# Softcap attention and a gated feed-forward layer: the gate as a tanh straight out of PSUM, gate and value units in turn, and outputs by chunks

## The chip, the cores and the metric

The kernel runs on one core of a Trainium2 chip. The core has engines that each work through a queue of their own in order: TensorE (PE; its weight loads are PEld in the profile), VectorE (DVE), ScalarE (ACT), GpSimd (POOL) and SyncE (SP), which here only issues DMAs. PE accumulates into banks of PSUM; ACT and DVE read these; everything else lives in SBUF. The metric is device time in microseconds.

## The reference

All arrays are float32, and the layer follows the attention directly:

```python
# q, k, v: (4, 12, 448, 64); w_gate, w_val: (768, 1536); w_out: (1536, 768)
scores = matmul(q, k.T) / sqrt(64)
scores = cap * tanh(scores / cap)               # cap = 30
attn = softmax(scores)
x = matmul(attn, v) -> (4*448, 12*64)           # tokens x model
gate = 1 / (1 + exp(-(x @ w_gate)))
val = x @ w_val
out = (gate * val) @ w_out                      # (1792, 768)
```

## The kernel before

Every float32 matrix is split into a high and a low half, and a product is three matmuls: high by low, high by high, low by high. A value that is made on the chip therefore passes two more engines before PE can use it: the high half is made by POOL or ACT (L174, L176), the low half, which subtracts it, by DVE (L182).

The attention takes a pair of heads at a time. PE transposes q and k (`tp`, L209 and L295), ACT copies them (`T`), PE makes the scores (`sc`, L325), ACT applies tanh to them (`t`, L328) and then exp (L336), ACT and DVE split the result (`ph`, `pl`), PE multiplies by v (`pv`, L366, L375 to L377). ACT copies parts of the product (`tmp`, L398), DVE adds (`xraw`, L400), POOL and DVE make the row sums (`a`, `as`), and DVE divides (`rd`). Six pairs make one batch of 448 tokens; DVE's `xspl` then holds its split x.

The feed-forward part of one batch, `moe(b)`, has 24 units h of 18 matmuls: 12 blocks of 128 columns of the gate and 12 of the values. Each unit ends in one of three PSUM banks. Then come two halves of the output, each of six units of w_out, with three chunks of 128 tokens that use the same three banks. The last 64 tokens of every batch are put off and done with the last batch (`rest`, `osr`).

The order of PE and ACT is the order of the program: the main loop takes turns between `moe(b)` and the attention of batch b+1, whichever is behind by its count of matmuls, so that a stretch of the profile holds both. A scheduler orders DVE, POOL and SP by dependences and by priorities (`tc.high_priority`). In the first such stretch the weights are also converted from 64-bit input by ACT and DVE (`pair`, L622 to L625) and written to DRAM; later batches load them back.

Around the change: the units are taken in three groups of four gate units and four value units. For a gate unit ACT copies the PSUM bank into a tile `gate` of four units (L749); after the fourth, one sigmoid goes over the whole tile (L755). For a value unit DVE multiplies the bank by the gate (L751), in the tile, and POOL and DVE split the product into `gspl` (L174, L182). The tile has one buffer, so the next group's first copy waits until the last low half of the old group is made. Tile `osb` of the output, three chunks wide, takes the same buffer. A sigmoid isn't in the table of functions that ACT holds for tanh and exp, so an `ACT_TABLE_LOAD` stands ahead of it, and another ahead of the next exp or tanh.

Of the kernel before, what the change touches and what calls it, by code (L numbers as in the profile page):

```python
# [9 lines left out]
F32 = mybir.dt.float32  # L10
# [5 lines left out]
AF = mybir.ActivationFunctionType  # L16
ALU = mybir.AluOpType
AX = mybir.AxisListType

P = 128  # L20
# [3 lines left out]
AHEAD_OF = 400  # L24
# [534 lines left out]
def _emit(tc, ctx, c, attention_of, q, k, v, w_gate, w_val, w_out, out):  # L559
# [3 lines left out]
    DFF = w_gate.shape[1]  # L563
    KD = DM // P
    KF = DFF // P
    NG = 3
    HM = DM // 2
    KU = 2
    W64 = 3
# [1 line left out]
    KEEP = 3  # L571
    AHEAD = 3
    WB = 4
    GF = KF // NG

    big = ctx.enter_context(tc.tile_pool(name="big", bufs=1))
    wp = ctx.enter_context(tc.tile_pool(name="wp", bufs=2))
# [5 lines left out]
    ap = o.ap  # L583
# [4 lines left out]
    UN = KD * P  # L588
    NU = 3 * KF
    src = []  # L590
    for g in range(NG):
        for w in (w_gate, w_val):
            for f in range(g * GF, (g + 1) * GF):
                src.append(w[:, f * P:(f + 1) * P].rearrange("(k p) f -> p k f", p=P))
    for t in range(2):
        wt = w_out[:, t * HM:(t + 1) * HM].rearrange("(k p) f -> p k f", p=P)
        for x in range(0, KF, KU):
# [103 lines left out]
    def next_w(u):  # L701
        if u < NU:
            convert_to(u + LEAD)
        split_w(u + AHEAD)
        load_to(u + WB)
        return w_spl.pop(u)

    def moe(b):
# [3 lines left out]
        def passes(ps, s):  # L712
            for kk in range(KD):
                rh, rl = xs[:, 0, kk, :], xs[:, 1, kk, :]
                wh, wl = (s[:, i, kk * P:(kk + 1) * P] for i in range(2))
                for i, (a, r) in enumerate(((wh, rl), (wh, rh), (wl, rh))):
                    nc.tensor.matmul(  # L717
                        ps, a, r, start=(kk == 0 and i == 0), stop=(kk == KD - 1 and i == 2)
                    )
                if kk % 2 == 1:  # L720
                    yield 6
# [13 lines left out]
                    )  # L735
                rest.append(r)
        u = u0
        for g in range(NG):
            gate = big.tile([P, GF, S], F32, tag="gate", name=f"gate{b}_{g}")
            for which in range(2):  # L740
                for j in range(GF):
                    f = g * GF + j
                    w = next_w(u)
                    u += 1
                    ps = ps_m.tile([P, S], F32, tag="m", name=f"h{b}_{which}_{f}")
                    yield from passes(ps, w)
                    gt = gate[:, j, :]
                    if which == 0:
                        nc.scalar.activation(gt, ps, AF.Copy)  # L749
                    else:  # L750
                        nc.vector.tensor_mul(gt, ps, gt)  # L751
                        o.hi("p", g_spl[:, 0, f, :], gt)
                        o.lo("v", g_spl[:, 1, f, :], gt, g_spl[:, 0, f, :])
                if which == 0:
                    nc.scalar.activation(gate, gate, AF.Sigmoid)  # L755
        moe1_done[b] = True
        flush_x()

# [19 lines left out]
        for t in range(2):  # L778
            acc = []
            for m in range(len(chunks)):  # L780
                if m < o.NF:
                    acc.append(ps_m.tile([P, HM], F32, tag="m", name=f"o{b}_{t}_{m}"))
                else:
                    acc.append(o.two_banks(f"o{b}_{t}_{m}")[:, 0, 0:HM])
            for x in range(0, KF, KU):
                w = next_w(u)
                u += 1
                for ps, g_of in zip(acc, chunks):
                    for kk in range(KU):
                        wh, wl = (w[:, i, kk * HM:(kk + 1) * HM] for i in range(2))  # L790
                        gh, gl = (g_of(i, x + kk) for i in range(2))
                        for i, (a, r) in enumerate(((gh, wl), (gh, wh), (gl, wh))):
                            nc.tensor.matmul(  # L793
                                ps, a, r, start=(x + kk == 0 and i == 0),
                                stop=(x + kk == KF - 1 and i == 2),
                            )
                    yield 3 * KU * HM / S
            to = out[:, t * HM:(t + 1) * HM]
            osb = big.tile([P, o.NF, HM], F32, tag="gate", name=f"osb{b}_{t}")
            for m, ps in enumerate(acc):  # L800
                if m == o.NF:
                    tag, bufs = o.out_tag
                    osb = ap.tile([P, NR // P, HM], F32, tag=tag, bufs=bufs, name=f"osr{b}_{t}")
                dst = osb[:, m % o.NF, :]
                if m % 2 == 0 or b < B - 1:

                    with tc.high_priority(offset=2 * AHEAD_OF):
                        nc.vector.tensor_copy(dst, ps)  # L808
                else:
                    nc.scalar.activation(dst, ps, AF.Copy)  # L810
                if m == o.NF - 1:
                    nc.sync.dma_start(
                        out=to[b * S:b * S + o.FULL].rearrange("(m p) e -> p m e", p=P), in_=osb
                    )
            if b == B - 1:
                ends = to.rearrange("(b s) e -> b s e", s=S)[:, o.FULL:]
                for m in range(NR // P):
                    nb = P // R
                    nc.sync.dma_start(out=ends[m * nb:(m + 1) * nb], in_=osb[:, m, :])


    MS = {mybir.EngineType.PE, mybir.EngineType.Activation}
# [59 lines left out]
```

## Time and profile before

| | |
|---|---|
| timed runs | 791.04, 793.67, 794.62 us; median 793.67 |
| the profiled execution | 791.81 us, of it a span of 789.5 us |
| busy in the span | PE 750.8 us (95%), DVE 472.6 (60%), ACT 398.6 (50%), POOL 198.0 (25%) |
| granted clock of PE | 0.983 of full speed on average |

The span has these stretches: to 85 us attention of batch 0 alone; then attention of batch b+1 beside the feed-forward part of batch b, from 85 to 278.7, to 451.1 and to 624.9 us; then the feed-forward part of the last batch, to PE's last matmul at 776.6; then the last outputs. In a row, an idle time in brackets is that of the row's engine just before it, with what ended it. A name such as `gate<-h` gives the tile written and the tile read, and x12 says that twelve instructions in succession are put together.

### The profile page before, as it was taken

What the parts mean: (1) busy time and instruction counts of PE and PEld (TensorE: products, weight loads), DVE (VectorE), ACT (ScalarE), POOL (GpSimd) and SP (SyncE); (2) the same over time, 40 slices, a digit from 0 to 9 for tenths busy, and PEclk for the clock granted to TensorE, in tenths of its full rate; (3) what the DMA queues carried; (4) which work ended last, traced back from release to release, by engine and by line L of the source; (5) the groups of instructions that cost most, each with busy time, mean ns of one, the idle gap of its engine ahead of it and who ended that gap; (6) DMA issues with size and microseconds to landing.
All of it is one profiled execution on the core that took longest, in us unless ns stands there. A gap on an engine that the chain in (4) does not pass through costs nothing.

```text
span 789.5 us, 10148 instructions
## 1 busy us (share of the span) xinstructions
PE 750.8 (95%) x3908; PEld 643.4 (81%) x3908; DVE 472.6 (60%) x525; ACT 398.6 (50%) x415; POOL 198.0 (25%) x211
## 2 busy tenths in 40 slices
PE   7999799999999999999999999999979999999993
PEld 4555587788777988887899988887879999999993
DVE  1689359888799948758798629667896011211000
ACT  6998377887756547674854256583830021010000
POOL 1133101020131325344465314434571000100000
PEclk9999799999999999999999999999999999999997
DMA  8777567999989876555577965543469866665521
GB/s 222 190 215 222 183 209 250 358 296 333 293 254 363 304 253 172 193 182 174 164 220 226 296 198 158 193 158 124 157 199 291 302 224 220 226 225 172 191 100 54
DMA packets 133170, 173.00 MB, mean 219 GB/s; under 512 B 86136, under 2 KB 111224, under 8 KB 133112
## 3 DMA queue, kind: packets, MB, share of 16 engines
q1 hardware_dynamic: 132184, 172.02, 67.9%
q8 instruction: 33, 0.54, 0.3%
q10 hardware_dynamic: 928, 0.23, 0.1%
q14 instruction: 25, 0.20, 0.1%
HBM read 135.27 MB, written 36.18 MB: 217 GB/s over the span
## 4 chain that ended last, share of the span: by engine, by line
PE 68%; DVE 15%; ACT 8%; issue 4%; POOL 2%; DMA 1%; SPq 0%; DVEq 0%; POOLq 0%; ACTq 0%
PE h L717 32%; PE o L793 19%; PE pv L366 6%; PE sc L325 5%; DVE pair L625 2%; DVE rd L418 2%; PE tp L209 2%; ACT t L328 2%; DVE wspl L182 2%; PE pv L375 1%; PE pv L376 1%; ACT gate L755 1%; DVE gspl L182 1%; ACT ph L176 1%; DVE pair L624 1%
## 5 line engine op out<-in xcount | busy, mean ns | idle before, releaser
L717 PE MATMUL h<-xspl,wspl 128*128 128x448 f32 x1728 | 380.2, 374 | 0.0
L717 PEld LDWEIGHTS h<-xspl,wspl 128*128 128x128 f32 x1728 | 323.8, 189 | 42.7 <-issue 15.0
L793 PE MATMUL o<-wspl,gspl 128*128 128x384 f32 x864 | 160.5, 340 | 1.1 <-DVE gate L751 0.8
L793 PEld LDWEIGHTS o<-wspl,gspl 128*128 128x128 f32 x864 | 151.8, 189 | 5.8 <-issue 3.5
L328 ACT ACTIVATE t<-sc,scale 112x896 f32<-112x896 f32 (+1 forms) x96 | 91.4, 1002 | 37.2 <-PE sc L325 36.7
L749 ACT ACTIVATE gate<-h 128x448 f32<-128x448 f32 x48 | 25.9, 542 | 156.8 <-PE h L717 97.0
L174 POOL TENSOR_SCALAR gspl<-gate 128x448 fp32r<-128x448 f32 x48 | 34.8, 724 | 204.8 <-DVE gate L751 204.8
L336 ACT ACTIVATE t<-t,capv 112x1792 f32<-112x1792 f32 (+1 forms) x48 | 85.7, 1789 | 0.4
L325 PE MATMUL sc<-T 64*112 64x448 f32 (+1 forms) x576 | 74.7, 387 | 9.6 <-DVE T L182 5.4
L366 PE MATMUL pv<-t,vo 112*128 112x448 f32 x192 | 78.6, 542 | 0.0
L325 PEld LDWEIGHTS sc<-T 64*112 64x112 f32 (+1 forms) x576 | 48.8, 180 | 34.9 <-issue 9.2
L418 DVE RECIPROCAL rd<-rd 128x448 f32<-128x448 f32 x24 | 70.8, 2951 | 0.3
L751 DVE TENSOR_TENSOR gate<-h,gate 128x448 f32<-128x448 f32 x48 | 29.5, 614 | 67.7 <-PE h L717 67.4
L348 POOL TENSOR_TENSOR a<-t 128x448 f32<-128x448 f32 x24 | 31.2, 1298 | 117.9 <-ACT t L336 90.2
L366 PEld LDWEIGHTS pv<-t,vo 112*128 112x128 f32 x192 | 35.4, 189 | 25.2 <-issue 24.6
L808 DVE COPY osb<-o 128x384 f32<-128x384 f32 x22 | 11.8, 553 | 72.6 <-PE o L793 72.5
L182 DVE TENSOR_TENSOR gspl<-gate,gspl 128x448 fp32r<-128x448 f32 x48 | 37.8, 788 | 24.3 <-POOL gspl L174 24.0
L182 DVE TENSOR_TENSOR pl<-t,ph 128x1344 fp32r<-128x1344 f32 x24 | 48.1, 2004 | 5.4 <-ACT ph L176 5.0
L176 ACT ACTIVATE ph<-t 128x1792 fp32r<-128x1792 f32 x24 | 40.7, 1697 | 18.1 <-PE pv L377 15.7
L623 DVE TENSOR_SCALAR pair<-pair 128x768 int32<-128x768 int32 x36 | 20.6, 573 | 38.7 <-ACT pair L622 37.2
L182 DVE TENSOR_TENSOR T<-tp,T 128x896 fp32r<-128x896 f32 (+1 forms) x24 | 26.9, 1121 | 25.7 <-ACT T L176 25.6
L622 ACT ACTIVATE pair<-w 128x768 f32<-128x768 f32 x36 | 32.5, 902 | 18.0 <-DVE wspl L182 12.1
(68 smaller groups left out, 728.2 us busy)
## 6 DMA issues: line engine op xcount, KB each, us to landing
wspl<-wd SPq DMA_DIRECT2D x111, 768.0 KB, 4.5
wd<-wspl SPq DMA_DIRECT2D x36, 768.0 KB, 5.3
w<-in_moe_w_gate_dram SPq DMA_DIRECT2D x12, 768.0 KB, 5.0
w<-in_moe_w_val_dram SPq DMA_DIRECT2D x12, 768.0 KB, 5.2
w<-in_moe_w_out_dram SPq DMA_DIRECT2D x12, 768.0 KB, 7.3
qk<-in_q_dram SPq DMA_DIRECT2D x46, 112.0 KB, 4.6
out_dram<-osb SPq DMA_DIRECT2D x8, 576.0 KB, 6.4
qk<-in_k_dram SPq DMA_DIRECT2D x22, 112.0 KB, 3.3
```

The costliest lines, as they stand in the source:

```text
L174: self.nc.gpsimd.tensor_scalar(dst, src, 1.0, 1.0, ALU.mult, ALU.mult)
L176: self.nc.scalar.activation(dst, src, AF.Copy)
L182: e.tensor_sub(dst, src, hi.bitcast(F32))
L325: nc.tensor.matmul(ps[0:w, j, 0:S], a[rows], r[rows], start=(i == 0), stop=(i == len(ops) - 1))
L328: nc.scalar.activation(Pt[n][0:w, :, m, :], ps[0:w, :, 0:S], AF.Tanh, scale=c["scale"][0:w])
L336: nc.scalar.activation(t, t, AF.Exp, scale=c["cap"][rows])
L348: nc.gpsimd.tensor_add(a, t[:, 0, :], t[:, 1, :])
L366: nc.tensor.matmul(pv, vs[n][0:QC, j * NC + m, :], Pt[n][0:QC, j, m, :], start=(m == 0), stop=(m == NC - 1),)
L418: nc.vector.reciprocal(rd, rd)
L622: nc.scalar.activation(x, top.bitcast(F32), AF.Copy, scale=2.0 ** -112)
L717: nc.tensor.matmul(ps, a, r, start=(kk == 0 and i == 0), stop=(kk == KD - 1 and i == 2))
L793: nc.tensor.matmul(ps, a, r, start=(x + kk == 0 and i == 0), stop=(x + kk == KF - 1 and i == 2),)
```

## The change

The sigmoid is written as (1 + tanh(x/2))/2, and tanh is in the table that ACT holds already. ACT reads a gate unit's bank once, with tanh and a scale of 0.5, and its tile holds one unit, with three buffers. DVE adds 1 and multiplies by the value unit's bank in one instruction, with raised priority. The factor 1/2 is applied when the output is copied out of PSUM. Units take turns, gate and value of the same block, and the weights are loaded in that order. The output's three chunks each have a tile of the ring `gate` and a DMA of their own.

```diff
-    for g in range(NG):
+    for f in range(KF):
         for w in (w_gate, w_val):
-            for f in range(g * GF, (g + 1) * GF):
-                src.append(w[:, f * P:(f + 1) * P].rearrange("(k p) f -> p k f", p=P))
+            src.append(w[:, f * P:(f + 1) * P].rearrange("(k p) f -> p k f", p=P))
...
-        for g in range(NG):
-            gate = big.tile([P, GF, S], F32, tag="gate", name=f"gate{b}_{g}")
+
+        for f in range(KF):
+            gate = big.tile([P, S], F32, tag="gate", bufs=3, name=f"gate{b}_{f}")
             for which in range(2):
-                for j in range(GF):
-                    f = g * GF + j
-                    w = next_w(u)
-                    u += 1
-                    ps = ps_m.tile([P, S], F32, tag="m", name=f"h{b}_{which}_{f}")
-                    yield from passes(ps, w)
-                    gt = gate[:, j, :]
-                    if which == 0:
-                        nc.scalar.activation(gt, ps, AF.Copy)
-                    else:
-                        nc.vector.tensor_mul(gt, ps, gt)
-                        o.hi("p", g_spl[:, 0, f, :], gt)
-                        o.lo("v", g_spl[:, 1, f, :], gt, g_spl[:, 0, f, :])
+                w = next_w(u)
+                u += 1
+                ps = ps_m.tile([P, S], F32, tag="m", name=f"h{b}_{which}_{f}")
+                yield from passes(ps, w)
                 if which == 0:
-                    nc.scalar.activation(gate, gate, AF.Sigmoid)
+                    nc.scalar.activation(gate, ps, AF.Tanh, scale=0.5)
+                else:
+                    with tc.high_priority(offset=AHEAD_OF):
+                        nc.vector.scalar_tensor_tensor(gate, gate, 1.0, ps, ALU.add, ALU.mult)
+                    o.hi("p", g_spl[:, 0, f, :], gate)
+                    o.lo("v", g_spl[:, 1, f, :], gate, g_spl[:, 0, f, :])
...
-            osb = big.tile([P, o.NF, HM], F32, tag="gate", name=f"osb{b}_{t}")
...
+                if m < o.NF:
+                    dst = big.tile([P, HM], F32, tag="gate", bufs=3, name=f"osb{b}_{t}_{m}")
+                else:
+                    dst = osr[:, m - o.NF, :]
                 if m % 2 == 0 or b < B - 1:
 
                     with tc.high_priority(offset=2 * AHEAD_OF):
-                        nc.vector.tensor_copy(dst, ps)
+                        nc.vector.tensor_scalar(dst, ps, 0.5, None, ALU.mult)
                 else:
-                    nc.scalar.activation(dst, ps, AF.Copy)
-                if m == o.NF - 1:
-                    nc.sync.dma_start(
-                        out=to[b * S:b * S + o.FULL].rearrange("(m p) e -> p m e", p=P), in_=osb
-                    )
+                    nc.scalar.activation(dst, ps, AF.Copy, scale=0.5)
+                if m < o.NF:
+                    at = b * S + m * P
+                    nc.sync.dma_start(out=to[at:at + P], in_=dst)
```

ACT's order in the feed-forward part of batch 1, from the end of the second group of gate units on, before (`h_0_6` is the gate unit of block 6):

```order
L749 ACTIVATE gate_1_2655<-h_0_6_2754 128x448
L749 ACTIVATE gate_1_2655<-h_0_7_2801 128x448
L755 ACT_TABLE_LOAD
L755 ACTIVATE gate_1_2655<-gate_1_2655 128x1792
L398 ACTIVATE tmp_0_2839<-pv_0_2808 64x448
L176 ACTIVATE ph_1_2842<-t_2535 128x1792
L328 ACTIVATE t_2769<-sc_2_2855,scale 128x2x448
L328 ACTIVATE t_2769<-sc_3_2863,scale 128x2x448
L176 ACTIVATE T_2904<-tp_2895 128x960
L336 ACT_TABLE_LOAD
L336 ACTIVATE t_2769<-t_2769,capv 128x1792
```

The same pair of heads in ACT's order after the change:

```order
L744 ACTIVATE gate_5_2770<-h_0_5_2773 128x448
L398 ACTIVATE tmp_0_2860<-pv_0_2827 64x448
L176 ACTIVATE ph_1_2863<-t_2552 128x1792
L328 ACTIVATE t_2788<-sc_2_2876,scale 128x2x448
L328 ACTIVATE t_2788<-sc_3_2884,scale 128x2x448
L744 ACTIVATE gate_6_2850<-h_0_6_2853 128x448
L176 ACTIVATE T_2923<-tp_2914 128x960
L336 ACTIVATE t_2788<-t_2788,capv 128x1792
```

Ahead of `tmp_0` there is one tanh of one unit where two copies, a table load and the sigmoid stood; another stands ahead of `T`, and no load stands ahead of the exp.

ACT's order one pair of heads later, before, where the third group begins:

```order
L415 ACTIVATE rd_2978<-dn_2975 128x448
L336 ACTIVATE t_2769<-t_2769,capv 128x1792
L328 ACTIVATE t_3003<-sc_0_3004,scale 128x2x448
L328 ACTIVATE t_3003<-sc_1_3012,scale 128x2x448
L749 ACTIVATE gate_2_3035<-h_0_8_3038 128x448
L398 ACTIVATE tmp_0_3075<-pv_0_3045 64x448
L176 ACTIVATE ph_1_3078<-t_2769 128x1792
L328 ACTIVATE t_3003<-sc_2_3091,scale 128x2x448
```

The same place after the change:

```order
L415 ACTIVATE rd_2998<-dn_2995 128x448
L744 ACTIVATE gate_7_2970<-h_0_7_2973 128x448
L336 ACTIVATE t_2788<-t_2788,capv 128x1792
L328 ACTIVATE t_3021<-sc_0_3022,scale 128x2x448
L328 ACTIVATE t_3021<-sc_1_3030,scale 128x2x448
L744 ACTIVATE gate_8_3053<-h_0_8_3056 128x448
L398 ACTIVATE tmp_0_3093<-pv_0_3063 64x448
L176 ACTIVATE ph_1_3096<-t_2788 128x1792
L328 ACTIVATE t_3021<-sc_2_3109,scale 128x2x448
```

The instruction of block 8 has kept its slot; it writes a tile of its own ring now, not the group's only one.

DVE's order before, in the feed-forward part of batch 2, where the last value units end and w_out begins (`gate_2` is the last group's tile, `h_1_9` the value unit of block 9):

```order
L751 TENSOR_TENSOR gate_2_4568<-h_1_9_4794,gate_2_4568 128x448
L182 TENSOR_TENSOR as_1_4846<-a_1_4841,as_1_4846 64x448
L182 TENSOR_TENSOR gspl_3843<-gate_2_4568,gspl_3843 128x448
L751 TENSOR_TENSOR gate_2_4568<-h_1_10_4826,gate_2_4568 128x448
L182 TENSOR_TENSOR gspl_3843<-gate_2_4568,gspl_3843 128x448
L751 TENSOR_TENSOR gate_2_4568<-h_1_11_4882,gate_2_4568 128x448
L182 TENSOR_TENSOR xspl_4904<-xraw_3908,xspl_4904 128x448 x4
L352 TENSOR_TENSOR a_0_4932<-a_0_4932 64x448
L182 TENSOR_TENSOR gspl_3843<-gate_2_4568,gspl_3843 128x448
L182 TENSOR_TENSOR pl_0_4928<-t_4760,ph_0_4927 128x1344
L182 TENSOR_TENSOR ph_0_4927<-t_4760,ph_0_4927 64x448
L400 TENSOR_TENSOR xraw_3908<-pv_1_4940,tmp_1_4968 64x448
```

The same place after the change:

```order
L400 TENSOR_TENSOR xraw_3939<-pv_0_4836,tmp_0_4869 64x448
L182 TENSOR_TENSOR pl_1_4873<-t_4568,ph_1_4872 128x1344
L182 TENSOR_TENSOR ph_1_4872<-t_4568,ph_1_4872 64x448
L747 SCALAR_TENSOR_TENSOR gate_10_4779<-gate_10_4779,h_1_10_4829 128x448
L182 TENSOR_TENSOR gspl_3871<-gate_10_4779,gspl_3871 128x448
L747 SCALAR_TENSOR_TENSOR gate_11_4859<-gate_11_4859,h_1_11_4916 128x448
L182 TENSOR_TENSOR xspl_4938<-xraw_3939,xspl_4938 128x448 x4
L182 TENSOR_TENSOR gspl_3871<-gate_11_4859,gspl_3871 128x448
L182 TENSOR_TENSOR pl_0_4962<-t_4797,ph_0_4961 128x1344
L182 TENSOR_TENSOR ph_0_4961<-t_4797,ph_0_4961 64x448
L400 TENSOR_TENSOR xraw_3939<-pv_1_4974,tmp_1_5002 64x448
L352 TENSOR_TENSOR a_0_4966<-a_0_4966 64x448
```

Block 9 is done earlier, two products stand ahead of the four `xspl`, and the sum `a_0` has moved behind the add L400.

## Rows read from the trace of the kernel before

**Rows 1.** Busy us of each engine (instructions), PEclk, DMA share, GB/s, by stretch.
```profile
85.00:278.70 193.70, 190.59 (x947) 155.00 (x947) 156.77 (x186) 130.64 (x149) 29.05 (x30) 0.99 0.86 285
278.70:451.10 172.40, 169.91 (x937) 152.99 (x937) 127.19 (x131) 96.76 (x94) 78.99 (x77) 1.00 0.64 207
451.10:624.90 173.80, 167.01 (x885) 151.36 (x886) 111.85 (x115) 85.65 (x84) 62.70 (x62) 0.98 0.61 195
624.90:776.60 151.70, 151.67 (x792) 143.16 (x791) 18.36 (x30) 14.79 (x20) 6.82 (x12) 1.00 0.57 190
776.60:789.50 12.90, 0.00 (x0) 0.00 (x0) 0.56 (x1) 0.00 (x0) 0.00 (x0) 0.61 0.20 68
```

**Rows 2.** Waits of PE, 85 to 625 us: us in total, times, longest.
```profile
PE tp L295 <- ACT t L328: 5.9, 6, 1.8
PE pv L375 <- DVE xraw L400: 4.3, 1, 4.3
PE sc L325 <- DVE T L182: 4.0, 1, 4.0
PE o L793 <- DVE gate L751: 0.8, 1, 0.8
PE sc L325 <- ACT rd L415: 0.7, 2, 0.3
```

**Rows 3.** Timeline around 370 us: start, duration, engine, line, tiles, [idle <- releaser].
```profile
366.78 1.49 PE L325 MATMUL sc<-T 64*128 64x448 f32 x12
...
370.12 0.55 ACT L749 ACTIVATE gate<-h 128x448 f32<-128x448 f32 x1 [10.76 <-DVE gspl L182]
...
372.85 1.91 ACT L328 ACTIVATE t<-sc,scale 128x896 f32<-128x896 f32 x2
...
373.91 0.66 PE L295 MATMUL tp<-ident,qk 128*128 128x128 f32 x4 [1.78 <-ACT t L328]
```

**Rows 4.** Timeline around 546 us.
```profile
546.34 0.66 PE L295 MATMUL tp<-ident,qk 128*128 128x128 f32 x4 [1.79 <-ACT t L328]
...
547.15 4.24 PE L717 MATMUL h<-xspl,wspl 128*128 128x448 f32 x12
```

**Rows 5.** A stretch behind a wait of PE, columns as in the first group.
```profile
546.30:551.40 5.10, 5.06 (x21) 4.63 (x22) 2.57 (x3) 3.86 (x4) 1.15 (x1) 0.67 0.09 37
```

**Rows 6.** Timeline around a sigmoid, 340 to 347 us.
```profile
340.11 1.28 ACT L755 ACT_TABLE_LOAD   x1
...
341.41 1.70 ACT L755 ACTIVATE gate<-gate 128x1792 f32<-128x1792 f32 x1
...
346.36 0.66 PE L295 MATMUL tp<-ident,qk 128*128 128x128 f32 x4 [0.36 <-ACT t L328]
...
347.16 2.67 PE L717 MATMUL h<-xspl,wspl 128*128 128x448 f32 x12
```

**Rows 7.** DVE's instructions ahead of the wait at 587.50 us.
```profile
578.45 4.25 DVE L182 TENSOR_TENSOR xspl<-xraw,xspl 128x448 fp32r<-128x448 f32 x4
582.74 0.87 DVE L352 TENSOR_TENSOR a<-a 64x448 f32<-64x448 f32 x1
```

**Rows 8.** PE's instructions from 587 us on.
```profile
587.50 0.44 PE L375 MATMUL pv<-pl,vs 128*128 128x448 f32 x1 [4.30 <-DVE xraw L400]
...
589.49 4.38 PE L793 MATMUL o<-wspl,gspl 128*128 128x384 f32 x18
...
595.15 3.31 PE L793 MATMUL o<-wspl,gspl 128*128 128x384 f32 x18
```

**Rows 9.** Groups by line and shape: busy us, mean ns, idle before, releasers.
```profile
L751 DVE TENSOR_TENSOR gate<-h,gate 128x448 f32<-128x448 f32 x48 | 29.5, 614 | 67.7 <-PE h L717 67.4
...
L417 DVE SCALAR_TENSOR_TENSOR rd<-rd 128x448 f32<-128x448 f32 x24 | 15.3, 636 | 2.1 <-ACT rd L415 1.2
```

**Rows 10.** SP's last DMAs, and a late stretch.
```profile
776.09 1.62 SPq L819 DMA_DIRECT2D out_dram<-osr  x2
...
781.00:785.00 4.00, 0.00 (x0) 0.00 (x0) 0.00 (x0) 0.00 (x0) 0.00 (x0) 0.50 0.14 52
```

More of the change, by code (lines that the diff above doesn't have):

```diff
@@ L565, in _emit @@
     KF = DFF // P
-    NG = 3
     HM = DM // 2
@@ L573, in _emit @@
     WB = 4
-    GF = KF // NG
     big = ctx.enter_context(tc.tile_pool(name="big", bufs=1))
@@ L802, in moe @@
                     tag, bufs = o.out_tag
-                    osb = ap.tile([P, NR // P, HM], F32, tag=tag, bufs=bufs, name=f"osr{b}_{t}")
-                dst = osb[:, m % o.NF, :]
+                    osr = ap.tile([P, NR // P, HM], F32, tag=tag, bufs=bufs, name=f"osr{b}_{t}")
+                if m < o.NF:
+                    dst = big.tile([P, HM], F32, tag="gate", bufs=3, name=f"osb{b}_{t}_{m}")
+                else:
+                    dst = osr[:, m - o.NF, :]
                 if m % 2 == 0 or b < B - 1:
                     with tc.high_priority(offset=2 * AHEAD_OF):
-                        nc.vector.tensor_copy(dst, ps)
+                        nc.vector.tensor_scalar(dst, ps, 0.5, None, ALU.mult)
                 else:
-                    nc.scalar.activation(dst, ps, AF.Copy)
-                if m == o.NF - 1:
-                    nc.sync.dma_start(
-                        out=to[b * S:b * S + o.FULL].rearrange("(m p) e -> p m e", p=P), in_=osb
-                    )
+                    nc.scalar.activation(dst, ps, AF.Copy, scale=0.5)
+                if m < o.NF:
+                    at = b * S + m * P
+                    nc.sync.dma_start(out=to[at:at + P], in_=dst)
             if b == B - 1:
@@ L818, in moe @@
                     nb = P // R
-                    nc.sync.dma_start(out=ends[m * nb:(m + 1) * nb], in_=osb[:, m, :])
+                    nc.sync.dma_start(out=ends[m * nb:(m + 1) * nb], in_=osr[:, m, :])
     MS = {mybir.EngineType.PE, mybir.EngineType.Activation}
```

## The prediction

> **What bounds the kernel now.** I read four views, from coarse to fine. First the busy time of each engine in stretches [rows 1]: TensorE (PE) works 190.59 of 193.70 us in the stretch in which attention for batch 1 runs beside the feed-forward part of batch 0, 169.91 of 172.40 and 167.01 of 173.80 us in the next two, all 151.70 us in the last, and none of the closing 12.90 us. Before 85 us there is attention alone, which the change doesn't touch. So PE is the bound, and a change that gives it no other matmuls can win only its idle time, 12.4 us in the three middle stretches, the time that the idling costs afterwards, and what the end takes. ScalarE (ACT) is at 56% to 49% in the last two mixed stretches and VectorE (DVE) at 74% to 64%: relief on them counts where PE waits for them, and nowhere else.
>
> Second, the waits of PE between 85 and 625 us [rows 2]: six transposes wait 5.9 us for ACT's score tanh (L328), one P·V group 4.3 us for a DVE add (L400), one group of scores 4.0 us for DVE at 85 us, and two short groups 0.8 and 0.7 us. The 4.0 us lies before the first gate and is not touched. Third, the timeline around the long ones [rows 3, 4, 6 to 8]. Fourth, the granted clock behind them [rows 5].
>
> **The change part by part.** PE keeps its matmuls in number, shape and order; only which unit a slot holds differs. I go through the waits.
>
> A, the gate buffer. In the kernel before, one tile holds four gate units, and the first copy of the next group waits until the last low half of the old group is made. The copy at 370.12 starts after 10.76 us of idle ACT, released by DVE [rows 3]; everything behind it in ACT's order is late, so the score tanh starts at 372.85 and PE, ready 1.78 us earlier, begins its transposes at 373.91. The same happens at 546.34 with 1.79 us [rows 4]. ACT was free at 359.4 (370.12 less 10.76). After the change the slot in ACT's queue is `gate_8<-h_0_8`, into a ring of three tiles, and it waits for the low half of unit 5, three pairs of units back. The wait that replaces it is PE's own: the unit itself, then the scores that PE finishes at 368.27 [rows 3]. Two score tanhs of 1.91 us from there end at 370.2, and PE would ask for the first transpose at 372.13 (373.91 less 1.78): 1.9 us of margin, so both waits go whole: 3.57 us. Behind the second the clock falls: the stretch 546.30 to 551.40 has a granted clock of 0.67, between the levels 1.2 and 2.4 GHz [rows 5], and twelve matmuls take 4.24 us [rows 4] where the same twelve take 2.67 at 347.16 [rows 6]. Without the idle before it that goes too: 1.57. A is 5.14 us (bounds: 0 and 5.14).
>
> B, the sigmoid's stop in ACT's queue. At 340.11 a table load of 1.28 us and a sigmoid over four units of 1.70 stand ahead of the scores' work [rows 6]; PE is 0.36 us late at 346.36. It happens again in the next batch, and twice 0.35 in front of scores that wait for ACT's copy L415 (the 0.7 of [rows 2]). What goes from the queue is 2.98 us before each of the four, and a tanh of one unit (taken at 0.55, as the copy that it replaces [rows 3]) stands in its place, with another ahead of T: 1.42 us gained, with margin (bounds 0 and 1.42). Nineteen table loads of the executed path go, 24.3 us at 1.28 each, and twelve sigmoids, 20.4 us at 1.70 [rows 6]; 48 copies become 48 tanhs of equal length. ACT's busy time falls from 398.6 to about 354, and only the 1.42 us of it, with part of C, is on PE's path. The sigmoid begins 1.30 us after its load did [rows 6], so a switch costs ACT 1.30.
>
> The Trainium skill ("ScalarE: Activation LUTs", section "What ACT_TABLE_LOAD costs") gives a load about 1283 ns, which these rows show (1.28), and adds a drain of about 1380 ns to each switch, which they don't show. By the page ACT would be relieved of 19 times 2.66, an estimated 51 us, by the rows of 19 times 1.30, 24.7 us; by the page I would count part C below whole (2.8), for a time of 781.3, by the rows two thirds of it.
>
> C, the stretch 85 to 279. Of the 5.9 us 1.61 fall here (5.9 less 3.57 and 0.72), in two waits; the 0.8 for the gate product and 0.4 of a smaller wait for ACT are here as well. They come behind sigmoids, through the weights' conversion, in which ACT and DVE take turns; DVE is 81% busy here [rows 1], so the cause may be DVE's load alone, which stays. Bounds 0 and 2.8; as the two ACT waits are over half of it, I take two thirds, 1.8.
>
> D, the change from h to o in batch 2. PE waits 4.30 us at 587.50, and behind that 18 matmuls take 4.38 us where the next 18 take 3.31 [rows 8], slowed as those of A were: 5.37 us in all. What PE waits for is DVE: four low halves of x (4.25 us), then a sum of 0.87, then a low half, the P split and the add [rows 7]. Before this the old order has four products and their low halves in one burst, and the high halves of the four x tiles, on GpSimd (POOL), stand behind theirs. In the new order two products remain there, and the sum `a_0` comes after the add (DVE's two excerpts in the section on the change). That takes 0.87 us plus about half of the 4.25 (the burst's wait for POOL) out of the chain: 3.0 us, my estimate between the bounds 0 and 5.37.
>
> What is added. DVE's product of two operands becomes one with an addition: 48 times 22 ns (636 by the nearest row, 614 before [rows 9]), 1.1 us of an engine with idle time, at nothing on the path; were all of it on the path it would be 1.1 us. It is put ahead of older DVE work, and what is queued behind it then waits for PE's value unit; see the second rival. The halving rides on copies that exist. SyncE (SP) issues 24 DMAs of 192 KB instead of 8 of 576: 16 more at about 0.4 us each by the issue rate of the closing rows (two in 1.62 us with a wait between them [rows 10]), 6 us over the span, on a queue with gaps. A tanh of the next batch now can wait for one third of the output tile, where a copy waited for all of it.
>
> The end. After PE's last matmul 12.90 us pass [rows 1]. The last two DMAs are issued at 776.09 within 1.62 us, and from 781 to 785 us the DMA engines are at 0.14 busy and move 52 GB/s [rows 10]. Two pieces of 192 KB, 393 KB, at that rate take 7.6 us, which is the end as seen. These two are unchanged; the big DMA runs beside them. I take 0, with bounds of -1 and +2 us: the pair finds the engines emptier, since two chunks leave before the whole did, or SP's two more issues (0.8 us) and as much again and a little for shared engines delay it.
>
> The Trainium skill ("DMA: Bandwidth & Descriptors", section "Rules for kernel authors") speaks against this part: it asks to coalesce many small transfers into a large one. By it the end grows and the time is that of the last rival below, 784.3; by the row the closing time is that of the pair that stays, and the sum takes nothing.
>
> **The sum.** 5.14 + 1.42 + 1.8 + 3.0 = 11.4 us. The profiled execution took 791.81 us (span 789.5 and 2.3 around it), so 780.4. The median of the three timed runs lies 1.86 us above the profiled one; I put the same on top: **782.3 us**.
>
> **The rivals.**
>
> All of it goes. If C gives 2.8, D 5.37 and the 0.2 us of another short wait go too, the gain is 14.9 and the time 778.8. For it: nothing else in the middle stretches idles PE. Against: DVE keeps nearly all its work, and D is a chain through DVE.
>
> The waits only move. ACT has slack already, so the next link of the same chains (DVE's low half of T, the add L400, POOL's sums) may be late in the same place. For it: 4.3 of the waiting is on DVE by name. Against: in A, the largest, the next link has 1.9 us of margin by the rows. With half of A and B and nothing else, the gain is 3.3 and the time 790.4; with A whole and nothing of D, 787.
>
> Slower: the product blocks DVE. DVE works in order, and a product with raised priority that DVE reaches before PE has finished the value unit holds everything behind it: low halves, adds, conversions on which PE waits a unit later. For it: DVE idled 67.7 us in front of these products already, 67.4 of it for PE [rows 9]. It decides from where a product is reached more than the slack of the work behind it too early. By the order, what PE needs from behind a product it needs about two units later, some 8 us (a unit is 18 matmuls, 18/12 of the 2.67 us in [rows 6]), so I hold it for unlikely. Price: in three mixed stretches there are 36 products; if one in two holds up PE by a quarter of a unit, 1.0 us, 18 us are lost and the time is 793.67 - 11.4 + 18 = 800. Slower than can be told from no change needs 15.4 us.
>
> The end grows. If the chunks push the closing pair back by the full 2 us, the time is 784.3; still faster.
>
> **How the numbers follow.** My forecast 0.55 (range of its own 779.5 to 787), all of it 0.14, the waits only move 0.20 (787 to 793), slower 0.06, a longer end 0.05. A measurement of this kernel can tell half a per cent, 4 us, so faster means below 789.7 and slower above 797.6. Faster: 0.55 + 0.14 + 0.05 and a third of 0.20, 0.80. Within: 0.14. Slower: 0.06. The range reaches from 776 (full gain, an end 1 us shorter, and the spread of the runs) to 792; what is outside is the blocked DVE, the moved waits' upper end and a little below.
>
> **What would show it.** Right: no transpose of PE waits over 0.5 us for L328 between 280 and 560 us, and ACT's gate rows wait for PE alone; one table load at the start and none after; ACT busy near 354 us; PE's busy time lower by about 2.6 us, since the slowed matmuls go; the wait near 587 about 2 us, with the clock behind it nearer to 1. Wrong: a new wait of PE for DVE in front of T or the add; PE rows for h waiting for a bank of PSUM that the product frees; an interval after PE's last matmul over 15 us. The forecast falls if the transposes keep their 1.8 us waits with another releaser.

## The result and the profile after

| | median of the timed runs | range | ratio to before (95% interval) |
|---|---|---|---|
| before | 792.97 us | 791.04 to 794.62 | |
| after | 786.22 us | 782.15 to 786.68 | 0.990 (0.9863 to 0.9936) |

The change makes the kernel 6.8 us faster by the medians; 11.4 were forecast, for 782.3 us. Both medians are of five executions; one of the changed kernel, at 937 us with a granted clock of 0.746, is left out of the range and the ratio, and without it the median is 785.83 us. The execution that was profiled took 786.68 us, of it a span of 784.9.

The busy line of the page after; that of before reads PE 750.8, DVE 472.6, ACT 398.6:

```profile
PE 754.0 (96%) x3908; PEld 647.0 (82%) x3908; DVE 476.3 (61%) x525; ACT 354.7 (45%) x384; POOL 196.3 (25%) x211
```

ACT lost the 44 us that were forecast. PE's busy time grew, where it should have fallen; the start, below, is why. The stretches of [rows 1] after the change, same columns:

```profile
90.30:281.20 190.90, 189.83 (x946) 155.37 (x946) 158.78 (x185) 118.69 (x140) 30.51 (x30) 0.98 0.87 290
281.20:450.60 169.40, 169.40 (x938) 153.30 (x936) 127.89 (x131) 83.95 (x85) 77.15 (x77) 1.00 0.67 213
450.60:621.20 170.60, 165.55 (x887) 149.97 (x886) 112.89 (x115) 72.78 (x75) 61.50 (x62) 0.99 0.62 198
...
773.00:784.90 11.90, 0.03 (x1) 0.00 (x0) 0.56 (x1) 0.00 (x0) 0.00 (x0) 0.60 0.12 39
```

The second mixed stretch has no idle PE left; the third has 5 us. The waits of PE from 90 to 625 us, to set beside [rows 2]:

```profile
PE sc L325 <- DVE T L182: 4.3, 1, 4.3
PE pv L375 <- DVE xraw L400: 2.7, 1, 2.7
PE pv L375 <- DVE pl L182: 1.3, 1, 1.3
PE dn L410 <- DVE as L182: 1.0, 1, 1.0
PE tp L295 <- ACT t L328: 0.7, 1, 0.7
PE o L787 <- DVE osb L804: 0.3, 1, 0.3
```

Of six transposes that waited for ACT one is left, in w_out of batch 0 (at 258.48 us). The waits for DVE in w_out of batch 2 have become three where there was one.

So that each part can be weighed, I cut the span at PE's first matmul of each h and each w_out phase, o; the number is that of the batch. The table has these lengths (us) for the profiled execution of every kernel that follows; "rest" is the span less the start.

| | start | h 0 | o 0 | h 1 | o 1 | h 2 | o 2 | h 3 | o 3 | end | rest |
|---|---|---|---|---|---|---|---|---|---|---|---|
| before | 86.91 | 134.62 | 57.07 | 124.18 | 48.25 | 124.92 | 48.78 | 89.27 | 62.57 | 12.93 | 702.6 |
| after | 92.21 | 134.32 | 54.67 | 121.17 | 48.23 | 120.32 | 50.25 | 89.27 | 62.57 | 11.87 | 692.7 |
| e1 ring only | 89.60 | 134.61 | 57.49 | 122.89 | 48.25 | 122.05 | 49.75 | 89.27 | 62.57 | 11.90 | 698.8 |
| e2 tanh only | 86.88 | 134.07 | 54.91 | 121.55 | 48.25 | 120.73 | 49.03 | 89.27 | 62.57 | 12.84 | 693.2 |
| e2d pass, no loads | 87.00 | 133.82 | 55.94 | 121.73 | 48.25 | 120.76 | 49.65 | 89.27 | 62.57 | 13.22 | 695.2 |
| e3 no priority | 92.09 | 134.29 | 54.77 | 121.16 | 48.23 | 120.32 | 50.29 | 89.27 | 62.57 | 11.81 | 692.7 |
| e4 one DMA | 89.60 | 133.70 | 54.95 | 121.16 | 48.83 | 120.32 | 50.34 | 89.27 | 62.57 | 12.26 | 693.4 |
| e6 x spread | 90.94 | 134.34 | 54.77 | 121.17 | 48.74 | 120.32 | 50.28 | 89.27 | 62.57 | 11.78 | 693.2 |
| e7 sigmoid in turn | 86.84 | 133.94 | 55.44 | 121.16 | 48.90 | 120.32 | 51.51 | 89.27 | 62.57 | 11.93 | 695.0 |
| e8 x held back | 90.83 | 134.34 | 53.10 | 121.16 | 48.25 | 120.33 | 44.95 | 89.27 | 62.57 | 11.90 | 685.9 |
| e8b the same in before | 90.63 | 134.22 | 60.02 | 124.16 | 48.25 | 123.48 | 45.22 | 89.27 | 62.57 | 12.97 | 700.2 |
| e9 e8 and filler | 90.06 | 134.33 | 53.10 | 121.16 | 48.25 | 120.33 | 44.95 | 89.27 | 62.57 | 11.88 | 685.8 |

The rest fell by 9.9 us; the start took back 5.3. But the start is not the change's. Kernels with nothing of the change have the long one too (e8b), and three with part of it have the short one (e2, e2d, e7). What differs is PE's clock, in the profile after between 10 and 30 us:

```profile
10.00:20.00 10.00, 8.10 (x43) 5.14 (x39) 1.09 (x1) 8.17 (x8) 0.00 (x0) 0.54 1.15 302
20.00:30.00 10.00, 9.51 (x35) 5.13 (x34) 0.71 (x1) 5.37 (x7) 0.00 (x0) 0.78 0.43 87
```

and before:

```profile
10.00:20.00 10.00, 7.56 (x42) 4.07 (x40) 1.09 (x1) 9.35 (x9) 0.00 (x0) 1.00 1.06 300
20.00:30.00 10.00, 9.51 (x48) 5.55 (x48) 4.60 (x6) 8.76 (x9) 0.85 (x2) 1.00 0.66 144
```

The granted clock is 0.54 and 0.78 in one, 1.00 in the other, for the same instructions. It goes with the start in all twelve profiles: from 10 to 20 us it is 1.00 in the four with a start of 86.8 to 87.0 us and 0.53 to 0.77 in the eight with 89.6 to 92.2. So single times of one kernel spread by 5 us and more, and small effects are read from the stretches, not from medians.

### The profile page after: what moved, and what is told of

Its sections match the earlier page's. It is cut to its first block, busy times and chain, and to the rows that moved or that the text cites. A ratio compares the mean times of both kernels' runs of the same rounds, so it can differ in the third digit from the quotient of the medians.

```text
span 784.9 us, 10196 instructions
## 1 busy us (share of the span) xinstructions
PE 754.0 (96%) x3908; PEld 647.0 (82%) x3908; DVE 476.3 (61%) x525; ACT 354.7 (45%) x384; POOL 196.3 (25%) x211
## 4 chain that ended last, share of the span: by engine, by line
PE 90%; DVE 5%; issue 1%; ACT 1%; POOL 1%; DMA 1%; POOLq 0%; DVEq 0%
PE h L714 46%; PE o L787 20%; PE pv L366 8%; PE sc L325 8%; PE tp L209 2%; PE pv L376 2%; PE pv L375 2%; ACT t L328 1%; POOL xspl L174 1%; DVE pair L622 1%; DMA w<-in_moe_w_out_dram 1%; PE tp L295 1%; PE warm L74 1%; PE dn L410 1%; PE pv L377 1%
## 5 line engine op out<-in xcount | busy, mean ns | idle before, releaser
L366 PE MATMUL pv<-t,vo 112*128 112x448 f32 x192 | 80.8, 555 | 0.0
L747 DVE SCALAR_TENSOR_TENSOR gate<-gate,h 128x448 f32<-128x448 f32 x48 | 29.5, 616 | 76.1 <-PE h L714 75.8
L182 DVE TENSOR_TENSOR gspl<-gate,gspl 128x448 fp32r<-128x448 f32 x48 | 39.5, 822 | 27.5 <-POOL gspl L174 27.5
L804 DVE TENSOR_SCALAR osb<-o 128x384 f32<-128x384 f32 x22 | 11.8, 553 | 72.6 <-PE o L787 72.5
L622 DVE SCALAR_TENSOR_TENSOR pair<-w,pair 128x768 uint16<-128x768 uint32 x36 | 39.7, 1102 | 0.2
```

Source lines behind the costliest of these rows:

```text
L182: e.tensor_sub(dst, src, hi.bitcast(F32))
L366: nc.tensor.matmul(pv, vs[n][0:QC, j * NC + m, :], Pt[n][0:QC, j, m, :], start=(m == 0), stop=(m == NC - 1),)
L622: nc.vector.scalar_tensor_tensor(half, low.bitcast(U32), 2.0 ** -29, half, ALU.mult, ALU.add)
```

## The experiments

Medians and ratios are against runs of the kernel before on the same chip.

**e1, the ring alone.** 790.31 us, ratio 0.9962 (0.9944 to 0.9981).

```diff
-gate = big.tile([P, GF, S], F32, tag="gate", name=f"gate{b}_{g}")
...
+gates.append(big.tile([P, S], F32, tag="gate", bufs=GF, name=f"gate{b}_{f}"))
...
-nc.scalar.activation(gate, gate, AF.Sigmoid)
+for gt in gates:
+    nc.scalar.activation(gt, gt, AF.Sigmoid)
...
-osb = big.tile([P, o.NF, HM], F32, tag="gate", name=f"osb{b}_{t}")
...
+    dst = big.tile([P, HM], F32, tag="gate", bufs=GF, name=f"osb{b}_{t}_{m}")
...
```

The output's chunks come with the ring here, each with a DMA of its own, as in the changed kernel.

> The kernel before, in its order of four gate and four value units and with the sigmoid, but the gate units in a ring of four tiles of one unit; after the fourth copy four sigmoids of one unit each (0.55 us by the copy of the same size, 2.2 in sum where one of 1.70 stood), and the output's chunks use the ring with a DMA each. My theory (the single gate buffer caused the two long transposes' waits): the waits of 1.78 and 1.79 us near 370 and 546 go, with the slow clock of 1.57 behind the second, and no gate copy waits for a low half; the small waits of 0.36 and 0.35 behind the sigmoids stay or grow by up to 0.5 each: 4 to 6 us faster than before. Rival (it is the sigmoid and its table loads that make ACT late there): the two waits stay at over 1.2 us and the time is within 2 us of before.

The copy that waited 10.76 us for DVE in [rows 3] now waits for PE, as its row in the timeline of this run says, and no transpose waits behind it:

```profile
369.50 0.54 ACT L751 ACTIVATE gate<-h 128x448 f32<-128x448 f32 x1 [6.33 <-PE h L717]
```

So the ring by itself is enough to take the two long waits away. It wins less than expected, 1.3 us in h 1 and 2.9 in h 2, because the four waits behind the sigmoid grew, from 1.42 to 2.50 us in sum: four passes take 1.98 us where one took 1.70, and the transpose behind them waits 0.63 instead of 0.36:

```profile
350.01 0.66 PE L295 MATMUL tp<-ident,qk 128*128 128x128 f32 x4 [0.63 <-ACT t L328]
```

Outside h 1 and h 2, o 2 is 1.0 us longer, with PE's long wait there at 4.73 us in place of 4.30, o 0 is 0.4 longer, and the end 1.0 shorter.

**e2, tanh alone.** 786.0 us, ratio 0.990 (0.9877 to 0.9923).

```diff
-nc.scalar.activation(gt, ps, AF.Copy)
+nc.scalar.activation(gt, ps, AF.Tanh, scale=0.5)
...
-nc.vector.tensor_mul(gt, ps, gt)
+nc.vector.scalar_tensor_tensor(gt, gt, 1.0, ps, ALU.add, ALU.mult)
...
-nc.scalar.activation(gate, gate, AF.Sigmoid)
...
-nc.vector.tensor_copy(dst, ps)
+nc.vector.tensor_scalar(dst, ps, 0.5, None, ALU.mult)
...
```

> The kernel before with the gate as tanh in place of each copy, the sum with 1 in the product, and the half at the output; order, the tile of four units with one buffer, priorities and DMAs as before. My theory: the four waits of 0.35 behind table load and sigmoid go (1.42 us) and part of what waits between 85 and 279 us (0 to 2.7), while both long transposes' waits of 1.8 us stay, being the buffer's: 1.4 to 4 us faster than before. Rival (relief of ACT by 45 us carries the gain): both long waits shrink below 1 us and it is 6 us or more faster.

The rival won. With the old order, one buffer and no ring, the time and the rest are those of the whole change within 0.6 us, though not stretch by stretch: h 1 and h 2 are 0.8 us longer than there and the end 1.0, o 2 is 1.2 shorter. The timeline of this run at the place of [rows 3]:

```profile
363.01 1.49 PE L325 MATMUL sc<-T 64*128 64x448 f32 x12
...
364.72 0.54 ACT L749 ACTIVATE gate<-h 128x448 f32<-128x448 f32 x1 [9.14 <-DVE gspl L182]
...
367.44 1.91 ACT L328 ACTIVATE t<-sc,scale 128x896 f32<-128x896 f32 x2
...
368.51 0.66 PE L295 MATMUL tp<-ident,qk 128*128 128x128 f32 x4 [0.18 <-ACT t L328]
```

The gate's tanh, in the copy's place, still waits 9.14 us for the buffer, yet PE waits 0.18 in place of 1.78. It starts 1.71 us after PE's scores begin, the copy in [rows 3] 3.34 after them: DVE makes the low half 1.6 us earlier against PE. Where this comes from shows in rows of before that I had not followed, from its timeline 20 us ahead of the wait:

```profile
348.43 1.28 ACT L336 ACT_TABLE_LOAD   x1
...
349.72 1.79 ACT L336 ACTIVATE t<-t,capv 128x1792 f32<-128x1792 f32 x1
...
351.66 1.16 POOL L348 TENSOR_TENSOR a<-t 128x448 f32<-128x448 f32 x1 [2.77 <-ACT t L336]
...
353.39 1.02 DVE L182 TENSOR_TENSOR gspl<-gate,gspl 128x448 fp32r<-128x448 f32 x1 [2.24 <-POOL gspl L174]
```

POOL waits 2.77 us for the exp, which comes behind the load, and DVE 2.24 us for the high half that POOL makes behind that; from 353.39 on DVE is busy until the low half of the wait, but for 0.46 us. The buffer wait and the sigmoid's stop were links of one chain; to take either away shortens it enough.

**e2d, the pass without the loads.** 786.29 us, ratio 0.9906 (0.988 to 0.9933).

```diff
 # as e2, and after the fourth tanh:
+if which == 0:
+    nc.scalar.activation(gate, gate, AF.Copy)
```

> As the run with tanh alone (order of before, one gate buffer), but after the fourth tanh a copy of the whole gate tile onto itself stands where the sigmoid stood (128x1792, about 1.70 us), so that of the sigmoid's stop only the two table loads (2.6 us in a group) are gone. Read by stretches of the trace, since the start differs between executions by up to 5 us: from the first h unit of batch 1 to the last of it 124.18 us before and 121.55 with tanh alone, for batch 2 124.92 and 120.73. Theory L (the loads made ACT late, the pass has room): 121.5 to 122.1 and 120.7 to 121.3, time within 1 us of tanh alone. Theory P (the pass over four units, on which the products wait, is as bad): 122.6 to 123.5 and 122.5 to 124, 2 us or more slower than tanh alone.

Theory L: h 1 and h 2 take 121.73 and 120.76, within 0.2 us of tanh alone, though a pass of 1.70 us over the four units stands where the sigmoid stood. Of the stop of 4.3 us the 2.6 of table loads made ACT late; for the pass there was room in these two stretches. Outside them the run is 1.8 us longer than tanh alone, 1.0 of it in o 0 and 0.6 in o 2, for which no run shows the cause.

**e7, a sigmoid in every turn.** 785.83 us, ratio 0.9907 (0.988 to 0.9935).

```diff
-nc.scalar.activation(gate, ps, AF.Tanh, scale=0.5)
+nc.scalar.activation(gate, ps, AF.Sigmoid)
...
-nc.vector.scalar_tensor_tensor(gate, gate, 1.0, ps, ALU.add, ALU.mult)
+nc.vector.tensor_mul(gate, ps, gate)
...
-nc.vector.tensor_scalar(dst, ps, 0.5, None, ALU.mult)
+nc.vector.tensor_copy(dst, ps)
...
```

> The changed kernel's order, ring, priority and chunks, but each gate unit is a sigmoid straight out of PSUM, with the product a plain one and no halving: the executed path has some 54 table loads (1.28 us each) instead of one. Theory (what the change is worth is ACT's freedom from the loads, the rest of it little): ACT's busy time rises by 69 us to about 424; 17 pairs of loads in the three mixed stretches, each a stop of 2.6 us, make ACT late in front of transposes and scores; 5 to 20 us slower than the changed kernel, at 790 to 805 us. Rival (the alternating order gives each load room, since the slack is two units): within 2 us of the changed kernel.

My theory was wrong. The run's groups by line show 56 table loads, where the changed kernel has one:

```profile
L744 ACT ACT_TABLE_LOAD x28 | 35.9, 1283 | 36.4 <-PE h L714 32.6 <-DMA out_dram<-osb 3.3
...
L336 ACT ACT_TABLE_LOAD x27 | 34.6, 1283 | 0.5
...
L821 ACT ACT_TABLE_LOAD x1 | 1.3, 1283 | 4.9 <-DVE scale L84 4.9
```

and yet h 1 and h 2 last 121.16 and 120.32 us, to 0.01 us what they last with tanh. ACT stands idle for PE ahead of many of them (32.6 us in the first row), so one load with one gate unit is caught up before PE needs ACT again. Only the w_out stretches are longer, by 2.7 us in sum with o 0 to o 2, and the rest by 2.3. So in h 1 and h 2 it was not the number of loads that cost time, but that two of them, a pass and the buffer's wait fell together behind a group. ACT's busy time rose from 354.7 to 427.8 us, by 73.1 us or 1.33 for each of 55 loads more. The Trainium skill ("ScalarE: Activation LUTs", section "What ACT_TABLE_LOAD costs") counts 2.66 us to a switch with its drain. No run here shows the drain: ahead of the ten loads at L755 of the kernel before, ACT is idle 0.2 us in all, and in [rows 6] the sigmoid begins 0.02 us after its load ends.

**e3, no raised priority.** 785.08 us, ratio 0.9889 (0.9867 to 0.9911).

```diff
-with tc.high_priority(offset=AHEAD_OF):
-    nc.vector.scalar_tensor_tensor(gate, gate, 1.0, ps, ALU.add, ALU.mult)
+nc.vector.scalar_tensor_tensor(gate, gate, 1.0, ps, ALU.add, ALU.mult)
```

> The changed kernel without the raised priority on the product. My theory (the priority decides nothing that PE waits for in the three mixed stretches, since the ring leaves two units of slack): time within 2 us of the changed kernel. Rival (the raised priority puts the last product ahead of the four low halves of x in batch 2 and so holds up DVE there): those low halves start before PE's last gate and value unit ends and the stretch of w_out in batch 2 is 1.5 us shorter than in the changed kernel (48.8 instead of 50.3). Other rival (products late without it): PE waits for products or banks, 3 us or more slower than the changed kernel.

Every stretch agrees with the changed kernel within 0.15 us. The last product stands ahead of the four low halves without it too. The priority does nothing that a stretch shows, neither good nor the harm of my slower rival.

**e4, one DMA for the last chunks.** 784.63 us, ratio 0.9885 (0.9856 to 0.9915).

```diff
+if b == B - 1 and m == 0:
+    osb = big.tile([P, o.NF, HM], F32, tag="xraw", name=f"osb{b}_{t}")
...
+if b == B - 1 and m < o.NF:
+    dst = osb[:, m, :]
...
+if b == B - 1 and m == o.NF - 1:
+    nc.sync.dma_start(
+        out=to[b * S:b * S + o.FULL].rearrange("(m p) e -> p m e", p=P), in_=osb
+    )
```

> The changed kernel, but the last batch's three output chunks in one tile with one DMA of 576 KB for each half, as before. From PE's last matmul to the end of the span it was 12.9 us before and 11.9 after. If the chunks' own DMAs, which leave earlier, are the cause: 12.8 to 13.0 again, 1 us slower than the changed kernel. Rival (something else in the order of the last copies): it stays at 11.8 to 11.9. All stretches before it as in the changed kernel, within 0.3 us.

Neither: the end lasts 12.26 us, where the seven kernels with chunks have 11.78 to 11.93 and the four with the old form 12.84 to 13.22. The one DMA brings back 0.4 of the 1.06 us; the other 0.7 stays open. What differs comes after the issue: in the kernels before, after, e2, e2d and e4 SP starts to issue the last pair 0.5 us before PE's last matmul ends, here after the change (PE ends at 773.02), to set beside [rows 10]:

```profile
772.54 1.62 SPq L814 DMA_DIRECT2D out_dram<-osr  x2
```

**e6 and e8, the split of x.** In the profile after, the place of [rows 7] reads, from DVE's and PE's instructions in one timeline:

```profile
571.20 0.62 DVE L747 SCALAR_TENSOR_TENSOR gate<-gate,h 128x448 f32<-128x448 f32 x1 [2.75 <-PE h L714]
...
571.78 4.26 DVE L182 TENSOR_TENSOR xspl<-xraw,xspl 128x448 fp32r<-128x448 f32 x4
...
576.50 1.55 DVE L182 TENSOR_TENSOR gspl<-gate,gspl 128x448 fp32r<-128x448 f32 x1 [0.46 <-POOL gspl L174]
...
580.10 0.62 DVE L400 TENSOR_TENSOR xraw<-pv,tmp 64x448 f32<-64x448 f32 x1
...
580.86 0.71 PE L375 MATMUL pv<-pl,vs 128*128 128x448 f32 x1 [2.68 <-DVE xraw L400]
...
588.50 0.47 PE L375 MATMUL pv<-pl,vs 128*128 128x448 f32 x1 [1.32 <-DVE pl L182]
...
594.85 0.47 PE L410 MATMUL dn<-as,ones 128*128 128x448 f32 x1 [1.04 <-DVE as L182]
```

The four low halves still stand in one piece, and DVE is late from there on. e6 moved the split in the program, one tile behind each w_out unit from the fourth: 784.6 us, ratio 0.9872 (0.9843 to 0.9902).

```diff
 moe1_done[b] = True
-flush_x()
...
+if t or x >= 3 * KU:
+    flush_x(1)
```

> The changed kernel with the splitting of the next batch's x moved: none right behind the last value unit, but one of the six tiles behind each w_out unit from the fourth on (the tiles are needed only when the next batch begins). My theory (the four low halves, 4.26 us in one piece, put DVE's queue behind PE's, and every later wait of that stretch follows from it): PE's three waits near 581, 588 and 595 us (2.7, 1.3 and 1.0 us) go with the slow clock behind the first, the w_out stretch of batch 2 falls from 50.25 to 44 to 46 us, and the time falls 4 to 6 us under the changed kernel. Rival (DVE is overloaded there whatever comes first: reciprocals of 2.95 us and splits): the waits move to other instructions and the gain is under 1.5 us. Other rival: the next batch begins late because the last tiles aren't split, and the gain is given back at 621 us.

One of the four low halves now stands by itself, but in the same place, and o 2 is as long as in the changed kernel (50.28 us), so the run says nothing on the theory. DVE's rows in it:

```profile
571.14 1.57 DVE L182 TENSOR_TENSOR xspl<-xraw,xspl 128x448 fp32r<-128x448 f32 x1
573.18 2.78 DVE L182 TENSOR_TENSOR xspl<-xraw,xspl 128x448 fp32r<-128x448 f32 x3 [0.47 <-POOL xspl L174]
```

DVE's order is the scheduler's, which here took up the ready low halves whatever their place in the program. e8 holds them by a dependence: the high halves go to ACT, whose order is written. 777.34 us, ratio 0.9793 (0.9767 to 0.9818).

```diff
-o.hi("p", xs[:, 0, p, :], xr[:, p, :])
+o.hi("a" if b > 0 and p < 4 else "p", xs[:, 0, p, :], xr[:, p, :])
...
-moe1_done[b] = True
-flush_x()
...
+if x == 4 * KU and b not in moe1_done:
+    moe1_done[b] = True
+    flush_x()
```

> The changed kernel, but the next batch's x is split only from the fifth w_out unit on, with the high halves of its first four tiles on ACT, whose written order holds the low halves back on DVE (in the run that only moved the split in the program, DVE took it up as soon as the tile was free, at the same place). In DVE's order the four low halves now stand behind both P splits and adds that PE waited for. Theory (the 4.26 us of low halves put DVE behind PE there): the waits of 2.7, 1.3 and 1.0 us near 581 to 595 us go, the w_out stretch of batch 2 falls from 50.25 to 44.5 to 46.5 us, and the time is 3 to 6 us under the changed kernel. Rival (DVE is late there in any order): 48.5 us or more. Other rival: the first h unit of the last batch waits for x, and what is gained is lost at its start.

The theory holds in the main: o 2 lasts 44.95 us in place of 50.25, o 0 1.6 less, and h 3 begins without a wait. PE's waits from 84 to 640 us in this run:

```profile
PE sc L325 <- DVE T L182: 4.3, 1, 4.3
PE pv L375 <- DVE pl L182: 1.4, 1, 1.4
PE sc L325 <- ACT T L176: 1.0, 1, 1.0
```

The first and the last of these rows lie before the first h. Of the three waits in o 2 those of 2.7 and 1.0 us are gone. The one for DVE's P split is not: DVE's reciprocal and the second add still stand ahead of that split:

```profile
581.65 0.47 PE L375 MATMUL pv<-pl,vs 128*128 128x448 f32 x1 [1.45 <-DVE pl L182]
```

So not every wait of that stretch follows from the low halves. The clock's fall behind the first wait is gone too. After the change it was 0.64 there (579.92 to 582.92 us); in e8 it is 1.00 over the first 36 us of o 2 (568.01 to 604.01).

The four low halves now come late, and three of them stand after the last add, at 591 us:

```profile
591.44 1.63 DVE L182 TENSOR_TENSOR xspl<-xraw,xspl 128x448 fp32r<-128x448 f32 x3
```

There they take 0.54 us each, with POOL idle, against 1.07 in the changed kernel, where POOL is busy throughout (4.26 of the 4.26 us), first with the high halves. So the edit does two things, it moves the low halves and it takes the high halves off POOL; no run parts the two.

**e8b, the same in the kernel before.** 789.45 us, ratio 0.9961 (0.9937 to 0.9985). The edit is e8's, on the old lines:

```diff
-o.hi("p", xs[:, 0, p, :], xr[:, p, :])
+o.hi("a" if b > 0 and p < 4 else "p", xs[:, 0, p, :], xr[:, p, :])
...
```

> The kernel before with nothing of the change, but with the next batch's x held back as in the best version so far (split from the fifth w_out unit on, high halves of its first four tiles on ACT). Theory (the wait near 587 us comes from the four low halves in DVE's queue and has nothing to do with gate or output): PE's wait of 4.30 us there falls under 1.5 us, the w_out stretch of batch 2 falls from 48.78 to 44 to 46 us, the h stretches stay at 124.2 and 124.9, and the kernel is 3 to 6 us faster than before. Rival (the burst of the last group's products is needed for the wait to go): 47.5 us or more there, less than 2 us faster.

The 4.30 us wait of [rows 8] falls to 0.55, and o 2 from 48.78 to 45.22 with gate and outputs as they were, as the theory says; a wait of 1.33 us for the P split stands behind it, as in e8. The rest falls by 2.4 us only, since o 0 grew by 3 us, where PE now waits for an output copy that DVE does behind three of the low halves. The longest of PE's waits, and DVE's rows ahead of the one of 3.2 us:

```profile
PE tp L295 <- ACT t L328: 4.8, 5, 1.8
PE sc L325 <- DVE T L182: 4.3, 1, 4.3
PE o L791 <- DVE osb L809: 3.2, 1, 3.2
```

```profile
255.92 1.68 DVE L182 TENSOR_TENSOR xspl<-xraw,xspl 128x448 fp32r<-128x448 f32 x3
257.52 1.01 DVE L809 COPY osb<-o 128x384 f32<-128x384 f32 x2
```

**e9, filler at the start.** 776.02 us, ratio 0.9779 (0.9755 to 0.9803). The edit stands on e8's.

```diff
 emit_T(0)
+for _ in range(6):
+    nc.tensor.matmul(fill[:, 0:P], c["ident"], c["ident"], start=True, stop=True)
```

> The best version so far (x held back) with six more matmuls of 128x128 that compute nothing needed, right behind the first transposes, where PE waits for the first scores' operand. To the first h unit it took 86.9 us in some executions and 89.6 to 92.2 in others, of any of these kernels; in the long ones PE's first matmuls run slowly for 2.3 us longer and the granted clock is 0.50 from 11 to some 22 us. Theory F (the clock falls because PE idles there): all executions are short at the start, 86.9 to 87.6, and the median falls 2 to 4 us under the version without. Rival (the start is set by something outside the program): both lengths occur as before and the median is within 1.5 us.

Its profile has the long start, 90.06 us, with a granted clock of 0.50 from 16 to 22 us, though the filler keeps PE busy in the gap near 7 us; its spans lie between 772.2 and 775.9, as wide as without the filler (773.3 to 776.7). The rival stands, by one profiled execution and these spreads; what sets the start is open. The median is 1.3 us lower than e8's, which was taken on another chip, and the spreads don't tell the two apart.

## Why the prediction was right, and where it was not

The direction and the range held: ACT's stops were on PE's path in the middle of the program, the product did PE no harm, and the rest of the span fell by 9.9 us where the sum said 11.4. Four terms make that up. That the sum came so near is in part luck: D was 4.5 us short, and A, B, C and the end gave 3.0 us more than they were taken at.

A and B, the waits in h 1 and h 2, were to give 6.56 us and gave 3.01 + 4.59 = 7.60. But step A named one owner where there were two. It laid the 1.78 us to the single buffer and kept the sigmoid's share apart as the 1.42 of B. e1 and e2 show that they are not parts that add: the ring alone gives 4.2 in these two stretches, tanh alone 6.8, both and the new order 7.6. The step that failed is the reading of [rows 3]: the row's releaser, DVE's low half, is the last link, and I did not follow that link back to the exp, and by it to the table loads 20 to 30 us earlier. The releaser is right, as e1 shows, and it is not the only thing whose removal ends the wait, as e2 shows.

C was taken at 1.8 of 2.8 and gave 0.30 + 2.40 = 2.70 in h 0 and o 0. By e2 it is all tanh's (0.55 + 2.16); the doubt that DVE's load alone kept these waits was unfounded. Two waits in o 0, 0.74 and 0.33 us, were left, and these went with e8.

D was to give 3.0 and lost 1.47. The step said that the shorter burst and the moved sum take 3.0 us out of DVE's chain. DVE did begin the low halves sooner, 0.9 us into the stretch where it was 2.5, and the first wait shrank by 1.62, from 4.30 to 2.68. That start is all that was won: the low halves took 4.26 us as before (4.25), so the half that I put down to a wait on POOL did not go, and from their end to the end of the add it is 4.7 us in both, since the low half of the gate's product took 1.55 us behind an idle 0.46 where it had taken 0.62. The moved sum (0.62 us) came right behind the add and so went into the next gap, and PE, there earlier, ran into the reciprocal of 2.95 and the P split: 1.32 and 1.04 more. The 0.7 us that are still missing lie in shorter stops around these two. My rival "the waits only move" held, here alone. Which part of the change did this is open: the ring with the chunks alone lengthens o 2 by 0.97 (e1), tanh alone by 0.25 (e2), the priority has no part (e3). e8 and e8b show what the term should have been about: 4.3 us of low halves that nobody needs for 50 us, and that stood in [rows 7].

The end was taken at 0 and gave 1.06, just beyond the -1 of its bounds. The Trainium skill's rule to coalesce transfers ("DMA: Bandwidth & Descriptors", section "Rules for kernel authors") is for small ones, and names those under 64 KB as mostly overhead. The chunks have 192 KB, and three DMAs in place of one did not lengthen the end (11.87 us against 12.93).

Of the smaller steps, the product takes 616 ns where 636 was allowed, and ACT's busy time came out at 354.7 for 354. The test that PE's busy time would fall was a bad one, since it moves with the clock at the start: 748.0 us in e7, 754.0 in the changed kernel.

## What to carry to other kernels

Where a row names a releaser, ask what that one was waiting for, until the chain reaches something that the change removes; two waits on one chain don't add. Here table loads cost nothing in h 1 and h 2 while ACT waited for PE, and most of what was won there where two met in one stop, so spreading them was worth nearly as much as removing them (a rest of 695.0 us against 692.7). When a wait is for an engine that works in order, list what it does in the 10 us before and ask of each instruction when its result is needed: here the best find, 6.8 us of the rest (692.7 to 685.9), was a split that could wait, with its high halves on ACT.

## What the runs showed of the hardware

The same first instructions ran at a granted clock of 1.00 in some executions and 0.53 to 0.77 (10 to 20 us) in others, whichever kernel it was, and in the one profiled execution of the program that kept PE busier in the first gap it fell all the same. The fall goes with a start of 89.6 to 92.2 us in place of 86.8 to 87.0, 3 to 5 us of a time. The low halves of x on DVE took 1.07 us each with POOL busy all the while (4.26 of 4.26 us, after the change) and 0.54 us with POOL idle (e8). A table load cost ACT 1.30 us, with nothing to be seen of a drain.
